# Mask table by matrix products instead of a round trip through DRAM, one full-array pair fewer, a new order table

## The chip, the core and the metric

The kernel runs on one core of one Trainium2 chip. The metric is the time on the device in microseconds (us). Five engines of the core work side by side, each on its own stream of instructions in order: TensorE (PE in the profile, its weight loads PEld), VectorE (DVE), ScalarE (ACT), GpSimd (POOL) and SyncE (SP). DMA transfers are issued from the queues of SP, POOL and ACT. TensorE writes its products to PSUM, eight banks of 512 float32 columns; ScalarE and VectorE take them from there to SBUF.

## The reference

Block-sparse attention is followed by an MLP block. Shapes: 4 batches, 8 heads, 768 tokens, head size 64; blocks of 32 tokens, so 24 blocks.

```python
scores = q @ k.T / 8
mask = |blk_i - blk_j| <= 1, or either block is the first or the last,
       or blk_j is one of 3 sampled blocks of blk_i
attn = softmax(where(mask, scores, -1e9));  x = attn @ v        # heads side by side: [4, 768, 512]

a1 = alpha1 * x + beta1
u = x + lam * (w_tok @ a1)                                     # w_tok: 768 x 768, over tokens
a2 = alpha2 * u + beta2
out = u + lam * (relu(a2 @ w_ch1) @ w_ch2)                     # 512 -> 2048 -> 512
```

The mask is the same for all batches and heads, and constant in each block of 32 x 32.

## The kernel before, in words

The 32 heads are worked in 16 pairs p (four per batch). Scores are made transposed, keys on the partitions, so that the values can be multiplied without a transpose of the attention. The scores of a pair are cut into nine units of 1024 PSUM columns; unit n = 9p + u. The kernel knows two ways to work a pair:

- **Full-array pairs**, p < NPE (5 before). The two heads go one after the other. Queries and keys are transposed on TensorE (`H`) and copied from PSUM (`hq`, `hk`) into `qx` and `kx`. Under the 64 rows of the head lie 24 more rows (`MB`, partitions 64 to 87): in `kx` an indicator of the token's block, in `qx` 0 or -400 for each block. A product over 88 rows (L585) gives score and mask at once, and the exponential of a masked score becomes 0.
- **Paired heads**, p >= NPE. Both heads are transposed by DMA (`tq`, `tk`, `dma_start_transpose` on SP) into one tile, head 0 on rows 0 to 63, head 1 on rows 64 to 127. A unit is four products over 64 rows (L595), two in each half of the array. The mask is laid on after the exponential: `m` (L613) takes the minimum of the exponentials and a table `maskT` of 0 and 65504, on VectorE.

The table `maskT` (128 x 3 x 768, f16) is made from the 24 mask rows in `qx[3]`: `M` (L493) turns them into 0 and 65504, `N` (L499) writes them to DRAM with each row 16 times, `O` (L506) reads the result back so that each partition gets its rows.

The order of all work is written out by hand in `ORDER`, a table of words that a search made. Each word issues one step, and every engine executes its share in that order (`pin_order`). The letters: `lq lk lv` loads of a pair (POOL), `F` and `held` marks that hold a load back until VectorE has passed a point, `cq ck cv` casts, `q` scores (word `q52:0`: unit 52, PSUM pair of banks 0), `e` exponential (L606, ScalarE), `m` minimum, `p` and `r` values (L619), `n` and `nt` normalisation (full-array and paired), `a b` scale and shift, `k` the token mixing (L721), `x` its addition (L730), `u U v` the transposed input of the MLP, `f` first MLP product (L787), `g` its Relu (`:a` on ScalarE L801, `:d` on VectorE L803), `h` second MLP product (L821), `o` last addition (L831), `s` store. `W w` transpose the token weights, `L S P B` prepare parameters, `z` (defined, but not in the table before) is a product of zeros that nobody reads. An engine's suffix is `:a` or `:d`.

Before the table runs a fixed opening: TensorE multiplies zeros (`zero`, L299), the first heads are transposed and the mask rows made.

Of the kernel before, what the change touches and what calls it, by code (L numbers as in the profile page):

```python
# [12 lines left out]
F16 = mybir.dt.float16  # L13
# [25 lines left out]
NPE = 5  # L39
# [19 lines left out]
r35 q39:3 e39 q36:0 k4:3 L2 x2 F27 lx1 e36 n7 ah6 q42:3 k5:2 e42 q37:2 ah7 bh7 bh6 B0 k6:0 q40:3 u2
x4 x5 e37 U1:2 e40 ck5:d k7:1 u5 u4 x6 u6 x7 q38:2 U2:7 p36:3 v1:a e38 u7 q41:0 v2:d U3:2 q43:3 p37  # L60
p38 e41 e43 v3:d f10:2 f11:5 f8:0 f14:4 g11:a g8:d S4 g14:a f9:5 f15:6 f12:1 S5 g10:d f30:7 f13:2
f31:0 f28:4 g9:a cq6:a S7 S6 g13:d g12:a g28:d g30:d f29:1 p39 p40 f2:2 g29:d f27:7 lx0 f26:4 cq5:a
S1 S0 g15:a lv5 lk6 g2:a f5:6 f24:5 f6:1 f25:2 tq5 tk5 N0 tq6 g5:a n8 g31:d g26:d f4:0 f3:6 f7:3
f0:4 g4:a cq8:a P4:a F28 S2 g24:d S3 ck6:d g25:d g3:a g6:d g27:a g0:d f16:2 f22:0 r40:5 r41 O0 lv8
g7:d F29 r42 r43 lq9 r44 g16:d g22:d f23:4 q52:0 n9 e52 tk7 tk6 q48:1 g23:d q47:3 tq7 f19:5 g19:d
e48 f1:4 a4 q53:0 e47 q51:1 f20:5 f17:6 f18:7 b4 g1:d e51 m51 cv5:d F30 lv6 k9:4 cv6:d e53 g20:a
g17:a lk9 g18:a m52 cv7:a m53 k8:5 x9 F31 x8 m47 cq9:a lv9 f21:0 q50:1 q49:3 e50 q45:2 e45 p51:1 p52
lq10 e49 g21:a p53 m48 lk10 P2:d F32 ck9:d ck8:a h0:3 nt17 F33 p48:2 P0:d m49 h1 m50 h2 tk8 q46:3
q58:2 q59:0 e46 e59 m45 p49 h3 p50 lv10 e58 u8:a ck10:a h4:6 cq10:a tq8 nt16 m46 h8:7 p45:4 p46 p47
tk9 m59 o0 P5:d h9 nt15 a5 m58 q62:0 q61:2 q56:1 h5 h10 h11 e62 m62 F34 F35 lq11 lk11 P7:d e61 e56  # L70
q57:2 s0 e57 q55:1 q60:0 F36 b5 tq9 cq11:d u9:d lv11 e60 o2 e55 m56 cv8:a h6 lq12 m57 h7 p57:7 p58
F37 m60 o1 F38 m61 p59 q54:2 q70:0 P6:d q69:1 e54 k10:6 ck11:d lk12 x10 F39 e69 e70 p60:5 m54 F40
nt19 m69 F41 p61 p62 h20:4 h21 nt20 lv12 q66:3 q65:0 q64:1 s2 m70 k11:5 m55 P3:a s1 tk10 tq10 U4 e65
x11 e66 e64 u10:a p54:0 p55 ck12:d p56 h22 nt18 q68:3 q67:0 a6 q76:1 p69:5 h23 p70 e68 b6 lq13
cq12:d m66 k13:7 e67 e76 m68 m67 p66:6 u11:a q63:1 q71:0 p67 lk13 p68 o5 F42 U5 tq11 tk11 k12:4 e63
h24:2 m65 m64 e71 x13 m63 x12 m71 nt22 h25 p63:7 u13:a ck13:a cv9:d p71 p64 s5 p65 lv13 cq13:a lq14
h26 nt23 F43 lk14 nt21 q78:0 q74:2 q72:3 a7 b7 h27 e78 e72 e74 k15:3 k14:6 x15 x14 u15:d h16:4 u12:a
u14:a U6 h17 ck14:a P1:d o6 cv10:d m74 h18 h19 q75:1 q80:0 q81:3 F44 F45 o4 lv14 U7 f45:5 f47:4 e80
e75 m80 g47:d lq15 f44:0 f46:1 f40:2 m78 g45:d g46:d g40:a e81 f43:4 f42:5 g43:d g42:a f41:1 q77:1
q79:3 q73:2 m75 F46 g44:a g41:d F47 m72 f33:0 f34:1 e79 g33:d f38:6 e77 m76 p75:7 f37:2 e73 m77 m73  # L80
g37:a p72:0 p76 p77 g34:d f52:5 f48:2 p73 p78:1 nt25 m79 g48:a g52:d p74 p79 g38:a p80 q86:1 q91:2
nt26 q82:3 e86 f54:1 nt24 e91 f59:0 s6 tq12 tk12 e82 g54:d cv11:d q89:1 m86 q85:2 f51:1 g59:d m81
e85 e89 lk15 g51:d f49:7 g49:d m85 cq15:d f56:0 f35:6 g56:a g35:a s4 f36:2 q84:2 q87:3 m91 m82 q83:0
g36:a lv15 f57:2 f53:3 e87 f39:6 f58:7 e84 e83 g57:a a8 g53:d m84 m83 g58:a m87 g39:a f55:5 g55:a
f63:0 g63:d f60:7 f32:6 p81:1 p82 p84:0 p85 g32:d g60:a p86 nt28 q98:3 q92:1 q93:2 e98 p83 nt27 m89
b8 f62:0 e93 e92 g62:a f61:6 f50:1 g50:d m98 g61:d m92 h36:7 h37 q88:1 q94:2 e94 e88 q90:0 e90 h38
h32:6 k17:4 p87:5 m93 m94 m88 x17 p88 p89 h33 q95:1 q96:0 nt29 a9 b9 cv12:a e95 e96 m95 k16:4 p93:2
x16 m90 k18:3 x18 p94 q105:2 q100:0 p95 p90:3 p91 e100 e105 p92 nt31 nt30 m105 h34 q97:0 ck15:d
q102:1 q107:2 h39 e97 m96 k19:0 m97 o9 p96:1 e102 x19 e107 tk13 tq13 s9 m102 p97 q110:1 q103:2 e110
p98 h35 nt32 p105:7 e103 q104:1 q99:0 o8 u16:a e99 a10 u18:d m103 q101:2 e101 e104 cv13:d b10 m99  # L90
u17:a m104 h40:6 h41 h42 h43 p102:4 p103 p104 q106:0 q111:1 h52:5 m101 o10 m107 m100 u19:a s8 k20:6
# [11 lines left out]
m121 k25:6 m130 p120:4 p121 p122 x25 h69 h70 h71 m133 nt40 a13 x24 b13 q131:3 q126:2 q128:0 u24:a
e131 k26:2 e128 k27:6 h88:7 x26 o17 e126 cv15:a m131 q129:1 q140:2 q136:0 e129 u26:d e140 e136 x27
m126 m129 h89 h90 p129:6 p130 p131 q127:2 m128 m136 nt43 e127 m127 q134:1 q132:0 h91 h84:5 u25:d
p126:4 o22 s17 p127 s22 e134 e132 p128 nt42 q138:3 q135:1 q142:0 h85 e138 m132 p132:4 h86 p133 e135
m134 e142 p134 U12 q137:3 q143:1 q141:0 m138 m140 nt44 h80:4 h87 m135 a14 m142 u27:a e137 m137 e143
e141 p135:6 p138:7 p136 q139:1 p137 b14 k28:0 m141 e139 m143 k29:2 p141:1 m139 nt45 x29 x28 p139
# [82 lines left out]
def kernel(  # L191
# [111 lines left out]
    for _ in range(2):  # L303
        zero(P, 6)
# [181 lines left out]

    rows = maskT[:, 0, :]

    @on("M")
    def _(_i):
# [393 lines left out]
```

## Time and profile before

| | us |
|---|---|
| median of 3 runs (lowest, highest) | 308.25 (306.98, 310.96) |
| profiled execution | 308.12 |
| its span, first to last instruction | 306.3 |
| TensorE busy | 297.5 |
| VectorE busy | 221.7 |
| ScalarE busy | 197.7 |
| GpSimd busy | 52.4 |

The span is taken from one profiled execution; the profiled execution's own time is 1.8 us longer than its span. Busy time is the union of the bars of an engine. The bars of consecutive matmuls overlap, and so do those of consecutive instructions of VectorE and ScalarE, so that the distance from start to start is the better price of an instruction in a row of its kind. "Idle before" in a group's line is the time in which the engine had nothing running ahead of these instructions, with what ended it.

### The profile page before, as it was taken

What the parts mean: (1) busy time and instruction counts of PE and PEld (TensorE: products, weight loads), DVE (VectorE), ACT (ScalarE), POOL (GpSimd) and SP (SyncE); (2) the same over time, 40 slices, a digit from 0 to 9 for tenths busy, and PEclk for the clock granted to TensorE, in tenths of its full rate; (3) what the DMA queues carried; (4) which work ended last, traced back from release to release, by engine and by line L of the source; (5) the groups of instructions that cost most, each with busy time, mean ns of one, the idle gap of its engine ahead of it and who ended that gap; (6) DMA issues with size and microseconds to landing.
All of it is one profiled execution on the core that took longest, in us unless ns stands there. A gap on an engine that the chain in (4) does not pass through costs nothing.

```text
span 306.3 us, 7729 instructions
## 1 busy us (share of the span) xinstructions
PE 297.5 (97%) x3267; PEld 193.3 (63%) x3294; DVE 221.7 (72%) x478; ACT 197.7 (65%) x259; POOL 52.4 (17%) x95
## 2 busy tenths in 40 slices
PE   8999999999999999999999999999999999999995
PEld 3677888665655675575667575656676675565443
DVE  4498999697879997789788983477888896234042
ACT  4899998837979985679767834558377861351200
POOL 4645653211425421202000000000000000000000
PEclk9999999999999999999999999999999999999999
DMA  6999999999998999533020236104010212300022
GB/s 150 173 242 217 153 202 205 185 184 173 145 144 163 206 100 184 97 89 52 3 54 2 80 67 151 57 7 55 2 36 35 62 28 44 113 2 0 0 103 105
DMA packets 48399, 31.18 MB, mean 102 GB/s; under 512 B 29020, under 2 KB 44140, under 8 KB 48364
## 3 DMA queue, kind: packets, MB, share of 16 engines
q0 software_dynamic: 16016, 15.47, 34.0%
q1 hardware_dynamic: 32132, 14.97, 22.5%
q8 instruction: 26, 0.43, 0.6%
q10 hardware_dynamic: 216, 0.24, 0.2%
q14 instruction: 9, 0.07, 0.1%
HBM read 31.45 MB, written 6.88 MB: 125 GB/s over the span
## 4 chain that ended last, share of the span: by engine, by line
PE 84%; DMA 9%; DVE 3%; issue 2%; ACT 1%; DVEq 0%; SPq 0%; ACTq 0%
PE psum L821 24%; PE psum L787 23%; PE psum L619 11%; PE psum L721 10%; PE psum L595 8%; PE psum L585 6%; DMA kx<-rel 3%; DMA v<-in_v_dram 3%; DMA uT<-ub 2%; PE psum L336 1%; DMA k2f<-in_k_dram 1%; ACT eT L606 1%; DVE x_sb L730 1%; DMA out_dram<-ot 1%; PE psum L462 0%
## 5 line engine op out<-in xcount | busy, mean ns | idle before, releaser
L606 ACT ACTIVATE eT<-psum 128x1024 f16<-128x1024 f32 x145 | 137.6, 1020 | 24.3 <-PE psum L595 19.0
L787 PE MATMUL psum<-uT,w1b 128*128 128x384 bf16 (+1 forms) x512 | 87.4, 326 | 0.5 <-DMA uT<-ub 0.4
L821 PE MATMUL psum<-w2b,hts 128*128 128x512 bf16 (+1 forms) x373 | 85.5, 370 | 1.7 <-issue 0.5
L787 PEld LDWEIGHTS <-w1b 128*128 128x128 bf16 x512 | 48.8, 98 | 34.4 <-issue 0.9
L613 DVE TENSOR_TENSOR eT<-eT,maskT 128x1024 f16<-128x1024 f16 x99 | 65.2, 684 | 5.3 <-ACT eT L606 5.0
L821 PEld LDWEIGHTS <-hts 128*128 128x128 bf16 x400 | 36.5, 98 | 37.4 <-issue 2.3
L801 ACT ACTIVATE hts<-psum,b1t 128x384 bf16<-128x384 f32 x64 | 35.1, 586 | 32.6 <-PE psum L787 31.6
L803 DVE TENSOR_SCALAR hts<-psum,b1t 128x384 bf16<-128x384 f32 x64 | 38.0, 613 | 20.9 <-PE psum L787 20.2
L619 PEld LDWEIGHTS <-eT 128*128 128x128 f16 x1152 | 43.3, 97 | 9.4 <-issue 1.7
L619 PE MATMUL psum<-vext,eT 128*128 128x65 f16 x1152 | 47.0, 193 | 0.0
L721 PE MATMUL psum<-a1p,wtokT 128*128 128x128 bf16 x576 | 36.3, 219 | 0.0
L831 DVE TENSOR_TENSOR ot<-x_sb,psum 128x512 f32<-128x512 f32 (+1 forms) x25 | 16.5, 662 | 27.0 <-PE psum L821 22.0
L721 PEld LDWEIGHTS <-wtokT 128*128 128x128 bf16 x576 | 33.4, 98 | 4.0 <-issue 1.3
L595 PE MATMUL psum<-qx,kx 64*128 64x256 bf16 x396 | 28.6, 271 | 0.6 <-DVE flag L420 0.3
L585 PE MATMUL psum<-qx,kx 88*128 88x512 bf16 (+1 forms) x120 | 26.9, 340 | 0.8 <-issue 0.6
L595 PEld LDWEIGHTS <-kx 64*128 64x128 bf16 x396 | 16.2, 94 | 11.6 <-issue 4.7
L730 DVE TENSOR_TENSOR x_sb<-x_sb,psum 128x384 f32<-128x384 f32 x32 | 17.3, 550 | 6.9 <-PE psum L721 6.7
L385 ACT CAST ub<-x_sb 128x384 bf16<-128x384 f32 x16 | 8.1, 519 | 17.3 <-DVE x_sb L730 12.8
L403 POOL DMA_DIRECT2D k<-in_k_dram x15 | 10.8, 719 | 28.8 <-DVE vext L387 10.8
L691 DVE TENSOR_TENSOR a1p<-x_sb,a_bc 128x768 bf16<-128x768 f32 (+1 forms) x17 | 15.3, 908 | 0.3
L654 DVE TENSOR_TENSOR x_sb<-psum,rcp 128x256 f32<-128x256 f32 x33 | 14.0, 424 | 1.1
L403 POOL DMA_DIRECT2D v<-in_v_dram x16 | 11.6, 728 | 13.3 <-ACT rel L385 6.6
(70 smaller groups left out, 162.0 us busy)
## 6 DMA issues: line engine op xcount, KB each, us to landing
out_dram<-ot SPq DMA_DIRECT2D x23, 256.0 KB, 2.4
v<-in_v_dram POOLq DMA_DIRECT2D x16, 192.0 KB, 5.5
k<-in_k_dram POOLq DMA_DIRECT2D x15, 192.0 KB, 5.5
q<-in_q_dram POOLq DMA_DIRECT2D x15, 192.0 KB, 6.1
w2b<-in_moe_w_ch_dram POOLq DMA_DIRECT2D x4, 512.0 KB, 9.9
w1b<-in_moe_w_ch_dram POOLq DMA_DIRECT2D x4, 512.0 KB, 11.6
wtk<-in_moe_w_tok_dram POOLq DMA_DIRECT2D x3, 384.0 KB, 10.3
mask_rows<-maskT SPq DMA_DIRECT2D x1, 576.0 KB
```

Source lines behind the costliest of these rows:

```text
L403: nc.gpsimd.dma_start(t[:], pair_ap(src, *batch(p)))
L585: nc.tensor.matmul(t[:, f : f + w], kx[h][0:KC, ts(jt, P)], qx[h][0:KC, c : c + w], start=True, stop=True,)
L595: nc.tensor.matmul(t[:, (2 * a + j) * TH : (2 * a + j + 1) * TH], kx[h][r, ts(2 * g + j, P)], qx[h][r, ts(th, TH)], start=True, stop=True,)
L606: nc.scalar.activation(eTs[n][:, c], t[:, c], AF.Exp, bias=EXPB, scale=SCALE)
L613: nc.vector.tensor_tensor(out=e, in0=e, in1=mask, op=ALU.min)
L619: nc.tensor.matmul(ops[key][:, t * VW : t * VW + D + 1], eTs[n][:, c : c + P], vext[n // NU % NV][:, a, jt, 0 : D + 1], start=(first and z ...
L721: nc.tensor.matmul(t[:, j, :], wtokT[:, s, ts(3 * g + j, P)], a1p[p][:, s, :], start=(s == 0), stop=(s == NT - 1),)
L730: nc.vector.tensor_tensor(out=sl, in0=sl, in1=tps.pop(i), op=ALU.add)
L787: nc.tensor.matmul(hps[i][:, 0:w], w1b[:, dk, ts(f, P)], uT[b][:, dk, hf * HS : hf * HS + w], start=(dk == 0), stop=(dk == 3),)
L801: nc.scalar.activation(hts[kk][:, f, :], t[:, 0:HS], AF.Relu, bias=b1t[:, f : f + 1], scale=1.0)
L803: nc.vector.tensor_scalar(out=hts[kk][:, f, :], in0=t[:, 0:HS], scalar1=b1t[:, f : f + 1], scalar2=0.0, op0=ALU.add, op1=ALU.max,)
L821: nc.tensor.matmul(cps[i][:, 0:w], hts[kk][:, nk, ts(m, P)], w2s[0][:, nk, lo : lo + w], start=(nk == 0), stop=(nk == 15),)
```

## The change

`NPE` becomes 4, so pair 4 is worked as paired heads. `M`, `N`, `O` and the DRAM tensor go. In their place `Y` multiplies, for each of the three key groups g, the indicator rows of `kx[3]` (24 x 128) with the mask rows of `qx[3]` (24 x 768) into PSUM (512 + 256 columns); `y` copies the result into `maskT`, on ScalarE as Relu(164 x + 65504), on VectorE as before. In the new table all three `y` stand on ScalarE. The opening has two more zero products of 128 columns, and the table has six `z` (three of 480, two of 256, one of 384 columns). The order table is another one throughout: it has nine more `m` (108), 43 groups of paired `q` in a row in place of 36, ten `g` more on ScalarE (74 of 128), two heads less through `H`, two more DMA transposes.

```diff
-NPE = 5
+NPE = 4
 ...
-    for _ in range(2):
+    for _ in range(4):
         zero(P, 6)
 ...
-    mask_dr = nc.dram_tensor("mask_rows", [S // 2, S], F16, kind="Internal").ap()
 ...
-    rows = maskT[:, 0, :]
-
-    @on("M")
-    def _(_i):
-        nc.vector.tensor_scalar(
-            out=rows[MB, :], in0=qx[3][MB, :], scalar1=-1.0, scalar2=F16MAX, op0=ALU.is_ge, op1=ALU.mult
-        )
-
-    @on("N")
-    def _(_i):
-        nc.sync.dma_start(
-            mask_dr.rearrange("(m i) w -> m i w", m=NBLK),
-            rows[MB, :].unsqueeze(1).broadcast_to([NBLK, BLK // 2, S]),
-        )
-
-    @on("O")
-    def _(_i):
-        nc.sync.dma_start(maskT[:], mask_dr.rearrange("(p g) w -> p g w", p=P))
+    @on("Y")
+    def _(g, j):
+        ups["Y", g] = t = psum[:, 2 * j * 512 : 2 * j * 512 + S]
+        for c, w in ((0, 512), (512, S - 512)):
+            nc.tensor.matmul(
+                t[:, c : c + w], kx[3][MB, ts(2 * g, P)], qx[3][MB, c : c + w], start=True, stop=True
+            )
+
+    @on("y")
+    def _(g, eng):
+        t = ups.pop(("Y", g))
+        if eng == "a":
+            nc.scalar.activation(maskT[:, g, :], t, AF.Relu, bias=F16MAX, scale=164.0)
+        else:
+            nc.vector.tensor_scalar(
+                out=maskT[:, g, :], in0=t, scalar1=-1.0, scalar2=F16MAX, op0=ALU.is_ge, op1=ALU.mult
+            )
```

The old table begins

```
lv0 lk1 lq1 lt1 q1:1 cq0 lq2 q2:0 q0:3 H1:5 hm0 hq1:d hk1:d e1 e0 cv0:d lv1 lk2 q3:1 q4:3 p0:5 cq1:d
```

and the new one, with its words around the mask table and the first paired units,

```
lv0 lq1 lk1 q0:2 cq0 q1:0 e0 lt2 q2:3 hm0 H1:2 lk2 e1 q3:2 hk1:d lq2 hq1:d e3 lt0 cv0:d z480:3
z480:3 z480:3 q8:0 e2 lv1 z256:2 q4:2 q5:1 cq1:d lt1 e4 F18 p0:7 p1 lq3 p2 p3 e8 p4 q7:2 ck1:d lv2
...
H7:0 L0 hk6:d lc4 e22 q16:3 lv4 p21 hk7:d e16 Y0:1 lw1 a0 p22 r22:5 r23 y0:a Y1:3 hq7:d r16 y1:a
...
n5 e30 q35:0 x1 q27:1 cq5:d e35 k0:5 b1 ck4:d e27 tk4 q31:3 x0 q33:0 e31 a2 k2:2 tq4 u0 e33 q32:3 u1
x2 q34:2 tq5 e32 q28:0 ck5:d k3:3 u2 e28 b2 U0:7 e34 x3 p27:1 p28 tk5 u3 p29 cv4:a p30 v0:d p31 U1:0
n6 r31:5 r32 v1:a r33 ah6 r34 r35 F23 bh6 lv7 q43:1 n7 q40:3 e43 k5:4 q42:0 lx1 B0 ah7 e40 lw3 bh7
...
m36 p41 e38 u6 p36:2 p37 u7 e45 q52:0 F24 m38 lq8 U3:3 e52 v3:d q47:2 lx0 p38 f12:3 e47 f15:0 g12:d
```

More of the change, by code (lines that the diff above doesn't have):

```diff
@@ L59 @@
[L59 to L91, printed above, removed]
@@ L103 @@
[L103 to L108, printed above, removed]
```

94 lines of the change are left out of this document (63 added, 31 removed).

## The prediction

> **What bounds the kernel.** First the page's busy lines, then busy time by stretch.
>
> ```profile
> PE 297.5 (97%) x3267; PEld 193.3 (63%) x3294; DVE 221.7 (72%) x478; ACT 197.7 (65%) x259; POOL 52.4 (17%) x95
> ...
> DMA  6999999999998999533020236104010212300022
> ```
>
> ```profile
> 7.00:32.00 25.00, 24.09 (x314) 17.51 (x313) 19.32 (x44) 23.59 (x28) 13.51 (x23) 1.00 1.17 208
> 32.00:57.00 25.00, 25.00 (x398) 20.36 (x396) 21.89 (x56) 22.35 (x25) 11.60 (x19) 1.00 1.12 183
> 57.00:82.00 25.00, 24.51 (x227) 15.38 (x224) 21.83 (x51) 17.67 (x32) 6.27 (x13) 1.00 1.22 178
> ```
>
> The columns after the length are TensorE, its weight loads, VectorE, ScalarE, GpSimd, clock, DMA share, GB/s. TensorE (PE) looks full everywhere, but each matmul's bar overlaps the next, so bars can't say what work is left out. I therefore read its timeline by starts.
>
> ```profile
> 6.97 2.77 PE L585 MATMUL psum<-qx,kx 88*128 88x512 bf16 x8
> 9.53 0.85 PE L336 MATMUL psum<-identb,rel 128*128 128x128 bf16 x6
> ...
> 167.51 0.66 PE L619 MATMUL psum<-vext,eT 128*128 128x65 f16 x16
> 168.10 0.61 PE L595 MATMUL psum<-qx,kx 64*128 64x256 bf16 x8
> 168.65 0.42 PE L619 MATMUL psum<-vext,eT 128*128 128x65 f16 x8
> ...
> 169.76 0.41 PE L619 MATMUL psum<-vext,eT 128*128 128x65 f16 x8
> 170.11 0.83 PE L595 MATMUL psum<-qx,kx 64*128 64x256 bf16 x12
> 170.87 0.82 PE L821 MATMUL psum<-w2b,hts 128*128 128x512 bf16 x3
> ```
>
> Starts of undisturbed steps give the price of each word of the order table: q of a full-array pair 0.436 us, q of a paired one 0.219, eight value matmuls 0.244, k 1.005, f 0.650, h 0.863 (0.437 at 256 columns), six transposes 0.335. Times their counts: f 128 steps 83.2, h 92 and 8 steps 82.9, values 35.1, k 32.2, q 99 x 0.219 = 21.7 and 45 x 0.436 = 19.6, transposes of 19 heads and tiles 6.4: 281.0 us. The first q starts at 6.97, the last matmul is over at 302.4, so 295.4 us hold 281.0 of work and **14.4 lost**. TensorE is the bound, and there are two losses to follow.
>
> The first 4.0 are lost before 56.4. The first three q's take 2.56 us from 6.97 (0.853 each, half speed), and ScalarE (ACT) cannot keep up:
>
> ```profile
> 10.86 15.79 ACT L606 ACTIVATE eT<-psum 128x1024 f16<-128x1024 f32 x17 [0.42 <-PE psum L585]
> ...
> 24.68 6.65 ACT L606 ACTIVATE eT<-psum 128x1024 f16<-128x1024 f32 x7
> ```
>
> One exponential e runs 0.916 us start to start in a row, unbroken here. Ahead of the table's word k0 stand 24 e's and a copy of 0.68: 22.7 us of ScalarE against 19.6 us of TensorE, a lead of 3.1. TensorE reached k0 at 30.42, having lost 30.42 - 6.97 - 19.6 = 3.8. So **lost = ScalarE's lead + 0.8** while ScalarE has no rest.
>
> The other 10.5 come later, most at changes between paired q (64 rows) and other work (128 rows). Sixteen values should take 0.49 and take 168.10 - 167.51 = 0.59; two q's should take 0.44 and take 0.55. Over the trace the change costs 0.095 each way: 36 groups of paired q, 72 changes, 6.8 us.
>
> **The change, part by part.**
>
> The mask by DRAM goes: M (0.35 us of VectorE, DVE), N and O (0.84 and 0.36 us of SP's queue, 576 KB each way). No row waits for maskT, because the first min comes at 77.6; TensorE gains nothing. If that cover were gone it would be the transfers' time: N was issued at 63.49, O at 70.62.
>
> In their place Y, three times 512 + 256 columns: 216 + 109 = 0.325 us each by the starts of those widths, 1.0 us of TensorE. The nearest row on 24 rows, L346 at half speed, has 0.51 for 384 columns, so 3.1 us is the other end; both lie under ScalarE's lead. The three copies y are all on ScalarE: 768 columns lie between 0.494 (512) and 0.916 (1024): 0.70 each (1.5 to 2.7 for three), 2.1 us, unhidden where ScalarE leads. Relu brings no load of tables: the trace has one such load in all, though exponentials and Relus alternate from 55 on. The six z stand while e's are awaited: 2336 columns, 1.0 us, in time that is lost anyway; without that cover they cost 1.0, or 1.9 at half speed. The two extra zero(128) (0.107 each) go into a gap of 0.39 (4.37 to 4.76) in which rel is awaited: nothing.
>
> Pair 4 becomes paired: 9 x (0.436 - 0.219) = 2.0 and twelve transposes (0.7) leave TensorE; four copies of 0.48 and two normalisations of 0.66 leave VectorE, three of 0.52 come, and so do nine mins:
>
> ```profile
> L613 DVE TENSOR_TENSOR eT<-eT,maskT 128x1024 f16<-128x1024 f16 x99 | 65.2, 684 | 5.3 <-ACT eT L606 5.0
> L595 PE MATMUL psum<-qx,kx 64*128 64x256 bf16 x396 | 28.6, 271 | 0.6 <-DVE flag L420 0.3 <-DVE x_sb L730 0.2
> L585 PE MATMUL psum<-qx,kx 88*128 88x512 bf16 x60 | 21.2, 397 | 0.8 <-issue 0.6 <-ACT eT L606 0.2
> ```
>
> 9 x 0.602 (start to start) = 5.4. The new table moves ten g's and some copies from VectorE to ScalarE, so VectorE's sum stays: 208.9 before, 208.4 after; ScalarE's goes from 185.8 to 190.4. TensorE's becomes 281.0 - 2.0 - 0.7 + 1.0 + 1.0 = 280.3. GpSimd issues the same loads in another order, with three more held copies (0.3 each); no entry of the list of waits has TensorE waiting for a load now.
>
> Two DMA transposes are added on SP, tk4 and tq4, with tq5 and tk5 behind them. Their first casts are done where the table's sum for TensorE is 28.4, so tk4 goes out near 28.4 + 6.97 + 3.9 = 39.3; the first word that needs both, q43, stands at 35.4 and comes near 46.3. Rows for such a transfer:
>
> ```profile
> 60.80 1.31 SPq L554 DMA_TRANSPOSE qx<-rel  x1
> 62.23 1.21 SPq L554 DMA_TRANSPOSE kx<-rel  x1
> ...
> 64.44 4.97 SPq L554 DMA_TRANSPOSE qx<-rel  x1
> ```
>
> They land 4.4 to 7.4 after the issue, and the chain of waits holds one for 8.24 (from 62.23). So tq4, issued one issue (1.3) later at 40.6, lands between 45.0 and 49.4: it costs 0 to 3.1. N's 576 KB, which stood between 62.23 and 64.44, are not there at 40; I take 0.
>
> **The sum.** Ahead of v3 the new table has 49 e's, three y's, one cv and one v on ScalarE: 48.4, against 44.9 of TensorE, a lead of 3.5, so 4.3 lost, and v3 comes at 6.97 + 44.9 + 4.3 = 56.2 with 235.4 left. Before, the same rest stands at 56.5: **-0.3**. In the rest 95 paired q's come in groups with 69 changes against 72: **-0.3**. At the end the two last adds follow each other, and the second waited 0.23 for an output buffer; now only one follows the last matmul: **-0.2**. Span 306.3 - 0.8 = 305.5. The profiled execution took 308.12, 1.8 more than its span (the median shown is 308.25), so **307.3 us**. The 17 changes of row count that the new table has ahead of v3 I cost at nothing, since ScalarE sets that stage; without that cover they are 17 x 0.095 = 1.6.
>
> Against the change speaks a rule of the Trainium skill (TensorEngine Tiling, Key Properties): a change of tiling mode, not merely of tile, drains TensorE. The 0.095 agrees. By the rule the Y's, on 24 rows, might each drain too, up to six changes or 0.6 us; no row here shows it, and the sum would be 307.9 if ScalarE's lead did not hide it.
>
> **Rivals.**
>
> Late transposes: q43 waits for tq4 at the long landing, and k, h and f behind it wait too. For it: a DMA share of 1.12 in that stretch. Against: no mask transfer beside it. 307.3 + 3.1 = 310.4.
>
> VectorE becomes the bound, the slower side: between the words H7 and lx0 (20.1 to 45.1 of TensorE's sum) it holds 31.4 us by mean durations, against 25.0. Before, its densest stretch (g4 to q56) held 25.7 against 20.0, yet TensorE lost only 2.1 from 70 to 90, as VectorE's operations overlap when none waits (a min takes 0.684, the next starts after 0.602). If the 6.4 are paid in full, 2.5 of them are in the sum already (ScalarE's lead grows from 1.0 to 3.5 there): 307.3 + 3.9 = 311.2. It decides from the point where the mins wait for their e's one by one, so that the overlap ends: with 0.602 per min and like prices for the rest the stretch holds 27.1, 2.1 over TensorE and less than ScalarE's 2.5; at the full prices VectorE is ahead of ScalarE.
>
> The clock opens sooner: the q's at 6.97 run at full speed. TensorE saves 3 x (0.853 - 0.436) and 0.05 on each of six transposes, 1.5, but ScalarE still sets the stage and starts 0.4 sooner: 306.9. The longer run of zeros speaks for it, a gap before rel against it. The Trainium skill (TensorE: Matmul & The Clock Gate, Part 1) has full speed after about 3.4 us of sustained work; here 3.2 us of zeros (1.19 to 4.37) did not bring it, and 3.4 might.
>
> The new table removes half of the losses, of 4.3 and 10.5: 307.3 - 7.4 = 299.9. Nothing in the sums shows where.
>
> The change may also do nothing: that the table comes early is worthless if pair 4 gains no time; that is 308.1.
>
> **Numbers.** Forecast 0.52 (306.3 to 309), which takes in doing nothing; late transposes 0.20; VectorE 0.18; clock 0.06; losses halved 0.04. The range reaches to the long landing and VectorE's price above, and below to the clock and 3 us more for a halved early loss and the spread of the runs (306.98 to 310.96): 303.8 to 312.0. A measurement tells about 2% here (302.1 and 314.4). Faster: 0.05, the last rival and a little; slower: 0.06, late transposes and VectorE at full price together (314.2) and a little; the same 0.89.
>
> **What would show it.** Right: first q near 7, v3 near 56, about 86 changes of 0.095, e's unbroken to 55. Wrong: TensorE idle ahead of q43 on kx or qx (transposes); VectorE at 95% from 28 to 55 with values waiting for mins (VectorE); q at 0.43 from 7 us on (clock); a span that differs after 57 by more than 1 us with none of these.

## The result, and the profile after

The changed kernel is slower: 311.89 us median of four runs (310.77 to 312.60) against 307.75 (four runs, 306.98 to 310.96) of the kernel before on the same chip, a ratio of 1.0132 with the 95% interval 1.0087 to 1.0177. Forecast were 307.3 us, 0.8 less than the profiled execution of before, and no difference of 2%. The profiled execution took 310.77 us with a span of 309.0, where the sum had 305.5. Line numbers of the changed kernel are one lower than before from L371 on, and two lower from L510 on (e is L604, paired q L593, f L785, h L819; full-array q L583).

The busy lines and the DMA line of the page of the changed kernel:

```profile
PE 298.5 (97%) x3308; PEld 191.7 (62%) x3308; DVE 221.6 (72%) x480; ACT 200.9 (65%) x269; POOL 53.8 (17%) x98
...
DMA  6999999999997996450167035520010022400012
```

Busy time by stretch, with the columns as before (TensorE, weight loads, VectorE, ScalarE, GpSimd, clock, DMA share, GB/s):

```profile
7.00:32.00 25.00, 24.40 (x350) 17.60 (x347) 19.32 (x49) 24.96 (x29) 15.21 (x24) 1.00 1.17 204
32.00:57.00 25.00, 23.87 (x410) 18.97 (x409) 23.72 (x53) 23.30 (x27) 8.13 (x14) 1.00 1.10 168
57.00:82.00 25.00, 23.49 (x189) 14.41 (x189) 20.89 (x53) 16.61 (x37) 9.00 (x17) 1.00 1.20 175
```

TensorE was full from 32 to 57 before; now 1.13 us of that stretch are bare of any matmul, and 1.51 of the next (0.49 before). Its timeline, read by starts as in the prediction, says where:

```profile
6.44 1.47 PE L583 MATMUL psum<-qx,kx 88*128 88x512 bf16 x8 [0.33 <-DVE qx L356]
7.75 0.50 PE L336 MATMUL psum<-identb,rel 128*128 128x128 bf16 x6
...
45.39 0.61 PE L593 MATMUL psum<-qx,kx 64*128 64x256 bf16 x8 [0.94 <-DMA qx<-rel]
...
58.70 4.08 PE L785 MATMUL psum<-uT,w1b 128*128 128x385 bf16 x24 [0.97 <-DMA w1b<-in_moe_w_ch_dram]
63.32 0.99 PE L785 MATMUL psum<-uT,w1b 128*128 128x384 bf16 x5 [0.54 <-DVE flag L419]
...
128.19 0.99 PE L785 MATMUL psum<-uT,w1b 128*128 128x384 bf16 x5 [0.76 <-ACT w1b L748]
...
158.90 1.47 PE L819 MATMUL psum<-w2b,hts 128*128 128x512 bf16 x6 [0.76 <-DVE ot L829]
```

These are five waits that the kernel before did not have (the idle time in brackets; start to start each loses some 0.17 more, and "loses" below counts that): q43 for its DMA transposes, f12 for the loaded weights, f19 for a bank that VectorE frees late (VectorE had waited 0.72 for w2b), f34 for a parameter step on ScalarE, h40 for an output buffer. The full-array q's run at 0.436 us from the first on (three in 6.44 to 7.75): the clock is open early. The groups that answer to those shown of before:

```profile
L611 DVE TENSOR_TENSOR eT<-eT,maskT 128x1024 f16<-128x1024 f16 x108 | 71.3, 685 | 7.9 <-ACT eT L604 7.7
L593 PE MATMUL psum<-qx,kx 64*128 64x256 bf16 x432 | 31.1, 271 | 0.9 <-DMA qx<-rel 0.9
L583 PE MATMUL psum<-qx,kx 88*128 88x512 bf16 (+1 forms) x96 | 20.0, 326 | 0.7 <-DVE qx L356 0.3
```

Work is as counted: nine more units of paired q, nine more mins. By the price of each word the changed table holds 280.34 us of TensorE (280.3 forecast) between 6.44 and 305.36, so 18.6 are lost, against 14.4 before and 14.5 forecast. The loss at the word f19 (63.3) is 7.6, where before it was 4.0 at 62.6; behind it 11.0 are lost against 10.5.

The queue of SP in the changed kernel, then that of GpSimd, around the first two waits:

```profile
37.22 1.32 SPq L552 DMA_TRANSPOSE kx<-rel  x1
38.65 3.46 SPq L552 DMA_TRANSPOSE qx<-rel  x2
42.21 1.97 SPq L552 DMA_TRANSPOSE kx<-rel  x1
```

```profile
34.01 0.57 POOL L444 DMA_DIRECT2D w1b<-in_moe_w_ch_dram  x1
44.57 0.34 POOL L400 COPY held<-flag 1x1 bf16<-1x1 bf16 x1 [9.99 <-DVE flag L419]
45.05 0.70 POOL L402 DMA_DIRECT2D v<-in_v_dram  x1
45.74 0.77 POOL L450 DMA_DIRECT2D w2b<-in_moe_w_ch_dram  x1
46.49 1.10 POOL L444 DMA_DIRECT2D w1b<-in_moe_w_ch_dram  x2
```

The four transposes tk4, tq4, tq5, tk5 are issued from 37.2 to 44.2; before, the first stood at 60.80. The load lv7 is held until VectorE passes the mark F23, 9.99 us long, and lx1, lw3, lw0, lx3 stand behind it on GpSimd's queue. So the last two weight loads for f (w1b) go out at 46.5, behind 512 KB of w2b, and land 9.6 and 11.5 us after their issue. f12 could start at 57.5 and starts at 58.7. In the kernel before, GpSimd's queue had them out by 38.1:

```profile
36.41 1.64 POOL L445 DMA_DIRECT2D w1b<-in_moe_w_ch_dram  x3
```

### The profile page after: what moved, and what is told of

Read it like the earlier page. It is cut to its first block, busy times and chain, and to the rows that moved or that the text cites. A ratio compares the mean times of both kernels' runs of the same rounds, so it can differ in the third digit from the quotient of the medians.

```text
span 309.0 us, 7798 instructions
## 1 busy us (share of the span) xinstructions
PE 298.5 (97%) x3308; PEld 191.7 (62%) x3308; DVE 221.6 (72%) x480; ACT 200.9 (65%) x269; POOL 53.8 (17%) x98
## 4 chain that ended last, share of the span: by engine, by line
PE 69%; DVE 6%; DMA 2%; ACT 1%; issue 0%; ACTq 0%; DVEq 0%; SPq 0%
PE psum L785 24%; PE psum L819 24%; PE psum L719 7%; PE psum L617 7%; PE psum L593 6%; DVE eT L611 2%; DMA kx<-rel 1%; DVE a1p L689 1%; DMA uT<-ub 1%; DVE x_sb L728 1%; DVE x_sb L652 1%; DVE ot L829 1%; DVE a1p L695 0%; ACT w1b L748 0%; DVE ub L386 0%
## 5 line engine op out<-in xcount | busy, mean ns | idle before, releaser
L604 ACT ACTIVATE eT<-psum 128x1024 f16<-128x1024 f32 (+1 forms) x145 | 136.9, 1029 | 38.9 <-PE psum L593 37.6
L819 PE MATMUL psum<-w2b,hts 128*128 128x512 bf16 (+1 forms) x400 | 90.9, 371 | 0.8 <-DVE ot L829 0.8
L785 PE MATMUL psum<-uT,w1b 128*128 128x384 bf16 (+1 forms) x512 | 86.7, 326 | 2.4 <-DMA w1b<-in_moe_w_ch_dram 1.0
L611 DVE TENSOR_TENSOR eT<-eT,maskT 128x1024 f16<-128x1024 f16 x108 | 71.3, 685 | 7.9 <-ACT eT L604 7.7
L785 PEld LDWEIGHTS <-w1b 128*128 128x128 bf16 x512 | 49.0, 98 | 37.5 <-issue 2.2
L799 ACT ACTIVATE hts<-psum,b1t 128x384 bf16<-128x384 f32 x74 | 40.7, 581 | 30.3 <-PE psum L785 29.5
L819 PEld LDWEIGHTS <-hts 128*128 128x128 bf16 x400 | 36.1, 98 | 37.5 <-issue 3.0
L617 PEld LDWEIGHTS <-eT 128*128 128x128 f16 x1152 | 42.3, 97 | 10.7 <-issue 2.3
L801 DVE TENSOR_SCALAR hts<-psum,b1t 128x384 bf16<-128x384 f32 x54 | 31.9, 613 | 22.9 <-PE psum L785 21.9
L617 PE MATMUL psum<-vext,eT 128*128 128x65 f16 x1152 | 46.2, 193 | 0.3 <-ACT eT L604 0.3
L593 PE MATMUL psum<-qx,kx 64*128 64x256 bf16 x432 | 31.1, 271 | 0.9 <-DMA qx<-rel 0.9
L593 PEld LDWEIGHTS <-kx 64*128 64x128 bf16 x432 | 17.6, 94 | 10.6 <-issue 5.8
L400 POOL COPY held<-flag 1x1 bf16<-1x1 bf16 x30 | 10.4, 348 | 74.4 <-DVE flag L419 74.4
L583 PE MATMUL psum<-qx,kx 88*128 88x512 bf16 (+1 forms) x96 | 20.0, 326 | 0.7 <-DVE qx L356 0.3
L652 DVE TENSOR_TENSOR x_sb<-psum,rcp 128x256 f32<-128x256 f32 x36 | 15.3, 424 | 1.2
L402 POOL DMA_DIRECT2D v<-in_v_dram x16 | 11.6, 724 | 10.5 <-DVE rel L386 5.1
```

The costliest lines, as they stand in the source:

```text
L402: nc.gpsimd.dma_start(t[:], pair_ap(src, *batch(p)))
L583: nc.tensor.matmul(t[:, f : f + w], kx[h][0:KC, ts(jt, P)], qx[h][0:KC, c : c + w], start=True, stop=True,)
L593: nc.tensor.matmul(t[:, (2 * a + j) * TH : (2 * a + j + 1) * TH], kx[h][r, ts(2 * g + j, P)], qx[h][r, ts(th, TH)], start=True, stop=True,)
L604: nc.scalar.activation(eTs[n][:, c], t[:, c], AF.Exp, bias=EXPB, scale=SCALE)
L611: nc.vector.tensor_tensor(out=e, in0=e, in1=mask, op=ALU.min)
L617: nc.tensor.matmul(ops[key][:, t * VW : t * VW + D + 1], eTs[n][:, c : c + P], vext[n // NU % NV][:, a, jt, 0 : D + 1], start=(first and z ...
```

## The experiments

The theory: the change costs what it was costed at, and the slowdown is made of waits for transfers that the new order puts late. The rivals: the three y's on ScalarE, the opening, or the fourth paired pair as such.

**The transpose earlier (a_tq).** The issue of tq4 moves in the table from behind k2 to right behind Y2.

```diff
-L1 Y2:0 lk7 e26 lw2
+L1 Y2:0 tq4 lk7 e26 lw2
...
-e31 a2 k2:2 tq4 u0 e33
+e31 a2 k2:2 u0 e33
```

> The changed kernel with one word moved: tq4, the DMA transpose of pair 4's queries, goes out right after the third product Y2 instead of after tk4 and k2. Late-transfer theory (the changed kernel is slow because transfers that its new table needs earlier land late): TensorE's wait of 1.1 us ahead of q43 and ScalarE's rest of 1.6 us at 45.8 vanish, and the time falls by 1.1 to 1.6 us against the changed kernel (ratio to before 1.008 instead of 1.013). Changes-of-row-count theory (the 17 changes and 6 of the Y's ahead of v3 are not hidden and cost 2.2 us): the wait vanishes but the time falls by 0.5 us at most. If tk4 lands later than tq4, the wait stays as it is under both.

Measured 313.59, 1.0179 (1.0137 to 1.0221): no gain, rather a loss. tq4 went out at 26.32, but q43 then lost 0.84 to kx, whose transpose tk4 still went out at 38.8: the wait stays, as the expectation allowed for a late tk4. It did not foresee the loss. In this profile the mark F23 is passed 1.0 us later than in the changed kernel, the two w1b loads go out 1.0 later, f12 loses 2.92 to them, and 6.83 us of half speed lie around the end of that wait. What makes the mark late is not shown.

**The weight loads earlier (a_w1).** lw3 and lw0 right behind lw2, ahead of the mark.

```diff
-lk7 e26 lw2 q29:1
+lk7 e26 lw2 lw3 lw0 q29:1
...
-ah7 e40 lw3 bh7 m43 q44:1 lw0 e42
+ah7 e40 bh7 m43 q44:1 e42
```

> The changed kernel with two words moved: lw3 and lw0, the last two loads of w1b, go out right after lw2 instead of behind the load lv7 that waits 10 us for a mark of VectorE. Late-transfer theory: issued near 35 instead of 46.5, w1b is there before f12, TensorE's wait of 1.0 us ahead of f12 vanishes and the time falls by about 1.0 us. Rival (the DMA engines are full until 100 us, share 1.1, so that an earlier load only pushes back another): the wait moves to a later load (v of pair 4, k of pair 5) and the time stays within 0.5 us.

Measured 316.12, 1.0277 (1.0230 to 1.0324). The wait of f12 went, as wanted, but the transposes now stand behind the weights. SP's queue and TensorE of this kernel:

```profile
38.65 9.12 SPq L552 DMA_TRANSPOSE qx<-rel  x2
```

```profile
49.16 1.04 PE L593 MATMUL psum<-qx,kx 64*128 64x256 bf16 x8 [4.70 <-DMA qx<-rel]
...
58.92 0.94 PE L593 MATMUL psum<-qx,kx 64*128 64x256 bf16 x8 [2.60 <-DMA kx<-rel]
```

The issue of tq4 and tq5 took 9.12 us in place of 3.46, q43 waited 4.70 and a later paired q 2.60. Neither expectation held: the time rose. With the weights issued first, the transposes wait; from 44.0 to 48.8 us the DMA engines are at a share of 1.21. Another place for the two loads, behind the transposes but ahead of the mark, was not tried. And around the end of each of the two long waits a stretch of TensorE at half speed begins, to which the last section comes back.

**The y's on VectorE (a_yd).** `y0:a y1:a y2:a` become `y0:d y1:d y2:d`.

> The changed kernel with the three copies y on VectorE instead of ScalarE. If ScalarE sets the pace from 7 to 57 us, as the sums of the prediction have it, its 2.1 us of y's go straight into the time: f12 starts about 2 us earlier and the time falls by 1 to 2 us, as far as the late transfers then do not hold q43 and f12 longer. If TensorE sets the stage with its changes of row count, nothing falls (0 to +0.5 us, since VectorE takes 2.1 us more).

Measured 313.11, 1.0188 (1.0151 to 1.0225). VectorE comes to them later; three full-array q's that reuse a bank wait for the copy on L502, idle 0.46, 0.47 and 0.58 us. q43 loses 1.72. Both branches of the expectation missed. Moving the y's off ScalarE does not help; what they cost there this run can't tell, since the new waits cover it.

**The opening alone (b_z4).** The kernel before with four zero products in place of two.

```diff
-    for _ in range(2):
+    for _ in range(4):
         zero(P, 6)
```

> The kernel before with four zero products of 128 columns in its opening instead of two, as the changed kernel has. In the profile of the changed kernel TensorE ran at full speed from 4.6 us on, in that of before from 10.3 us. If the two zeros bring this, the profile here shows the clock at full speed from about 4.6 us, the first q near 6.4 with 0.44 us per q, and the time falls by 1 to 2 us. If it is the phase of a free-running window, the profile may show either, and the median falls by less than 0.5 us.

Measured 308.00, 1.0014 (0.9985 to 1.0042). The clock opened at 5.40 us in place of 10.26, and the first q's ran at 0.44 us each; the time stayed, where the expectation had 1 to 2 us less. That fits the sum of the prediction, in which ScalarE sets that stage.

**The broadcast loads left out (a_nolc, b_nolc).** In both kernels the loads of alpha1, beta1 and alpha2 are replaced by ones that GpSimd writes.

```diff
+        if 0 < i < 4:
+            nc.gpsimd.memset(t[:], 1.0)
+            return
```

> The changed kernel with less for the DMA engines early: the broadcast loads of alpha1, beta1 and alpha2 (256 KB each, between 15 and 27 us) are left out, and GpSimd writes ones there, so these parameters are not the given ones. Nothing else moves. DMA-room theory (the DMA engines are full until 60 us, four transposes take 8 us of them from 38 on, and q43 and f12 wait for what comes late): 0.77 MB less are about 4 us of DMA work at 190 GB/s, so the waits ahead of q43 (1.1) and f12 (1.0) vanish or halve, and the time falls by 1.5 to 3 us (ratio to before about 1.004 to 1.008). If the loads are late only because the load lv7 waits for its mark, f12's wait stays and the time falls by 1 us at most. If TensorE's changes of row count or ScalarE's copies are the cause, nothing falls.

> The control for it: the kernel before with the same three broadcast loads left out (ones written by GpSimd instead). In before no work of TensorE waits for a load ahead of 57 us, its first transposes by DMA go out at 60.8. All theories: ratio 0.997 to 1.003.

Measured: the changed kernel 310.72, 1.0091 (1.0060 to 1.0123); the kernel before 308.87, 1.0018 (0.9978 to 1.0057). With fewer bytes ahead, f12 no longer waits; q43 still loses 1.46 and f19 1.23. The control stayed, as expected; the changed kernel's gain is below the expected one, and its interval overlaps that of the changed kernel. So bytes are part of f12's wait, and q43's does not hang on them.

**The four weight loads together behind lv7 (a_lw).** The order on GpSimd's queue becomes lv7, lw3, lw0, lx3, lx1, all still behind the mark F23.

```diff
-F23 bh6 lv7 q43:1 n7 q40:3 e43 k5:4 q42:0 lx1 B0 ah7 e40 lw3 bh7 m43 q44:1 lw0 e42 x5 k4:7 u5 lx3 e44
+F23 bh6 lv7 lw3 lw0 lx3 lx1 q43:1 n7 q40:3 e43 k5:4 q42:0 B0 ah7 e40 bh7 m43 q44:1 e42 x5 k4:7 u5 e44
```

> The changed kernel with four loads in another order behind lv7: lw3 and lw0 (the rest of w1b) first, then lx3 and lx1 (w2b), instead of lx1, lw3, lw0, lx3. They go out at the same time as in the changed kernel, after the transposes of pairs 4 and 5. DMA-room theory: w1b lands earlier by about one load of 512 KB (2 to 2.6 us), f12's wait of 1.0 us vanishes, q43's stays, and the time falls by about 1 us, to a ratio near 1.010. Rival: S2 on VectorE, which needs lx1, now holds f19 longer (0.7 us now), and nothing is won.

Measured 309.40, 1.0062 (1.0026 to 1.0099), span 306.8. GpSimd's queue and TensorE of this kernel:

```profile
45.01 0.35 POOL L400 COPY held<-flag 1x1 bf16<-1x1 bf16 x1 [9.98 <-DVE flag L419]
...
46.19 1.10 POOL L444 DMA_DIRECT2D w1b<-in_moe_w_ch_dram  x2
47.27 1.52 POOL L450 DMA_DIRECT2D w2b<-in_moe_w_ch_dram  x2
```

```profile
45.24 0.61 PE L593 MATMUL psum<-qx,kx 64*128 64x256 bf16 x8 [0.34 <-DMA qx<-rel]
...
57.16 0.42 PE L617 MATMUL psum<-vext,eT 128*128 128x65 f16 x8
57.54 2.79 PE L785 MATMUL psum<-uT,w1b 128*128 128x385 bf16 x16
```

The waits of f12 and f19 are gone although the two w1b loads go out only 0.3 us earlier: 512 KB of w2b no longer stand ahead of them, and they land 5.9 and 7.8 us after their issue in place of 9.6 and 11.5. The gain is larger than expected; f19's wait went too. It was measured again beside the changed kernel (c_lw below).

**Pair 4 transposed on TensorE (a_pet, a_pet_lw).** tq4 and tk4 go; six plus six transposes (A, as in the opening) and two copies on VectorE (D) take their place, without and with the loads' move of a_lw (there A8 stands ahead of A9).

```diff
-ck4:d e27 tk4 q31:3
+ck4:d e27 q31:3
...
-k2:2 tq4 u0
+k2:2 u0
...
-e34 x3 p27:1 p28 tk5
+e34 x3 A9:4 D9:d p27:1 p28 A8:6 D8:d tk5
```

> The changed kernel with pair 4 transposed on TensorE (twelve transposes into PSUM, 0.7 us, and two copies of 0.5 us by VectorE) instead of by DMA; it stays a paired pair. DMA-room theory: two of the four early DMA transposes go (about 4 us of the DMA engines), q43 waits for nothing, pair 5's transposes and w1b come earlier, f12's wait vanishes, and the time falls by 1.5 to 2.5 us (ratio near 1.006). If paired work of pair 4 costs more than the sums say for another reason (mins on VectorE, changes of row count), the time stays or rises by up to 1 us.

> The changed kernel in the better order of loads (ratio 1.006), with pair 4 transposed on TensorE instead of by DMA. DMA-room theory: q43's wait (0.5 to 1.1 us) goes, against 0.7 us of transposes and 1.0 us of copies on VectorE, which has no room there either: ratio 1.003 to 1.008. If the profile has the clock open near 14 us again, as in the run without the new order of loads, about 1.5 us are due to that.

Measured 313.76, 1.0195 (1.0121 to 1.0270), and 310.05, 1.0062 (1.0030 to 1.0094). The second is no better than a_lw at 1.0062: q43's wait goes, but the transposes wait 0.80 for a bank that e frees, and two U's behind them wait 0.34 and 0.20 for VectorE. So q43's wait was not bought off with TensorE's time here. a_pet missed its expectation: f12 still waits, 1.74 us. (Its profile has the clock opening at 13.97 us; its lowest run, 312.93, is still above the changed kernel.)

**All waits that the profile names (a_best).** a_lw, and two late moves: the stores s6 and s4 ahead of tq12 on SP's queue, P0 on VectorE.

```diff
-f45:4 m76 P0:a f41:0
+f45:4 m76 P0:d f41:0
...
-q90:3 m89 m78 tq12 h34 e79 p81:2 s6 tk12
+q90:3 m89 m78 s6 s4 tq12 h34 e79 p81:2 tk12
...
-nt28 s4 m79 q92:0
+nt28 m79 q92:0
```

> The changed kernel with w1b's rest ahead of w2b as in the run before it (ratio 1.006), and with two later waits taken away: the stores s6 and s4 go out on SP ahead of tq12, which held them back until 153 us so that o8 and h40 waited (0.95 us), and P0 is on VectorE, so that f34 does not wait for ScalarE, which stands behind a cast held by a DMA transpose (0.57 us). Theory that the loss is a sum of such single waits: the time falls by another 1.3 to 1.5 us, to a ratio of 1.001 to 1.002. If a wait removed there is only paid at the next step, it stays near 1.006.

The reason for the late moves is in SP's queue of the changed kernel: the stores stand behind the transpose tq12. That one waits 27.6 us, until 152.5, for q79, the last product that reads the tile it writes. So the buffer that o8 needs, and with it h40, comes late.

```profile
152.51 1.21 SPq L552 DMA_TRANSPOSE qx<-rel  x1
153.82 0.53 SPq L838 DMA_DIRECT2D out_dram<-ot  x1
```

Likewise f34 waits for P0 on ScalarE, which stands behind the cast cq14, and that waits 2.57 us for a DMA transpose to release its tile. Measured 308.28, 1.0018 (0.9987 to 1.0049): as fast as the kernel before, no faster.

**The two edits apart and together, beside the changed kernel.** The four corners on one chip, against 308.91 us of the kernel before: c_after is the changed kernel as it stands, c_lw has the loads' move alone, c_late the late moves alone, c_both both.

> The changed kernel unchanged, beside the other three corners. Theory of two separate causes (loads behind lv7 near 45 us, queue waits near 127 and 158 us): 1.011 to 1.014. Rival, that the differences between earlier calls were the chip and the call: 1.005 to 1.008, like the loads' move alone.

> The four weight loads directly behind lv7, nothing else. Theory of two separate causes: 0.006 to 0.008 below the changed kernel of this call (the two waits of 1.0 and 0.7 us at 57 and 62 us gone, some half-speed windows with them). Rival: no more than 0.003 below it.

> Only the later moves: the stores s6 and s4 ahead of tq12, P0 on VectorE in place of ScalarE. Theory of two separate causes: the waits of 0.9 us ahead of f34 and 0.9 us ahead of h40 go, 0.004 to 0.006 below the changed kernel of this call, and the wait of 1.0 us ahead of f12 stays. Rival: the late waits only move to the next word that needs the same transposes, 0 to 0.002 below it.

> Both edits. Theory of two separate causes: their gains add, 0.010 to 0.013 below the changed kernel of this call, within 0.003 of the kernel before. Rival, that each edit removes a loss that the other would have hidden: no more than the better of the two alone.

| | median us | ratio to the kernel before (95%) |
|---|---|---|
| c_after | 312.23 | 1.0105 (1.0056 to 1.0154) |
| c_lw | 309.60 | 1.0029 (0.9993 to 1.0065) |
| c_late | 310.44 | 1.0062 (1.0026 to 1.0099) |
| c_both | 308.52 | 1.0010 (0.9976 to 1.0045) |

The loads' move takes away 0.0076 and the late moves 0.0043, each as expected; both take 0.0095, just short of the 0.010 expected. Their sum would be 0.0119, which the intervals can't tell from 0.0095. Each of the two gains by itself, and together they make up nearly all of the 0.0105; that their gains add up in full is not shown, for the step from c_lw to c_both, 0.0019, is within the noise. TensorE's timelines of c_late (line numbers one lower again) and of c_both:

```profile
62.30 4.08 PE L784 MATMUL psum<-uT,w1b 128*128 128x385 bf16 x24 [1.31 <-DMA w1b<-in_moe_w_ch_dram]
...
126.78 8.13 PE L784 MATMUL psum<-uT,w1b 128*128 128x384 bf16 x49
```

```profile
45.38 0.61 PE L593 MATMUL psum<-qx,kx 64*128 64x256 bf16 x8 [0.57 <-DMA qx<-rel]
...
57.66 10.66 PE L785 MATMUL psum<-uT,w1b 128*128 128x385 bf16 x64
```

c_late keeps f12's wait and has 49 f products in a row where f34 had waited; c_both has 64 in a row from f12 on, and keeps a wait of 0.57 ahead of q43.

**The mask products alone (b_Y).** The kernel before, still with five full-array pairs, gets Y and y near 50 us in place of M, N and O.

```diff
-p31 e32 M0 a2
+p31 e32 a2
...
-e40 ck5:d k7:1 u5 u4 x6 u6 x7 q38:2
+e40 ck5:d Y0:3 k7:1 Y1:2 y0:a u5 u4 x6 Y2:3 y1:a u6 x7 y2:a q38:2
...
-f25:2 tq5 tk5 N0 tq6
+f25:2 tq5 tk5 tq6
...
-r40:5 r41 O0 lv8
+r40:5 r41 lv8
```

> The mask part alone: the kernel before with its own table and five full-array pairs, in which M, N and O are replaced by the three products Y and three copies on ScalarE, put near 50 us. TensorE has 1.0 us of products and six changes of row count (0.6) more; ScalarE's 2.1 us fall where it has rest; SP and the DMA engines lose two transfers of 576 KB at 63 to 75 us, beside the first DMA transposes. If the products are what makes the changed kernel slow: ratio 1.005. If the time of TensorE is all that counts: +1.6 us at most, less what the freed transfers give back at the waits near 81 us (0.9 us): ratio 1.000 to 1.005.

Measured 310.48, 1.0056 (1.0019 to 1.0093). TensorE's loss by 60 us grew from 3.9 to 7.4. In it are 3.41 us at half speed from 54.56 and, as these lines of TensorE's timeline show, waits that come from the place of the words and not from their price:

```profile
51.44 0.49 PE L492 MATMUL psum<-qx,kx 24*128 24x512 bf16 x2 [0.78 <-ACT eT L604]
...
54.37 0.88 PE L583 MATMUL psum<-qx,kx 88*128 88x256 bf16 x3 [0.58 <-ACT maskT L500]
```

So the products bring nothing by themselves to a kernel whose mask by DRAM was not waited for. How much of the 1.7 us is their work and how much their place is not separated. Five of the twelve runs have a mean clock of 0.994, as one such half-speed stretch would give; their median is 311.06, that of the other seven 309.28.

**The four pairs without the products (a_dram).** The order of a_lw, the mask through DRAM as before: M and N at Y0's place, O at y2's.

```diff
-p21 hk7:d e16 Y0:1 lw1 a0 p22 r22:5 r23 y0:a Y1:3 hq7:d r16 y1:a
+p21 hk7:d e16 M0 N0 lw1 a0 p22 r22:5 r23 hq7:d r16
...
-L1 Y2:0 lk7
+L1 lk7
...
-k1:4 y2:a n5
+k1:4 O0 n5
```

> The changed kernel in the better order of loads (ratio 1.006), with the mask table through DRAM again: M and N in the place of Y0, O near the place of y2, so four full-array pairs without the products. ScalarE has 2.1 us less in the stage that it paces, TensorE 1.6 us less. DMA-room theory: two transfers of 576 KB at 28 to 45 us take room from the loads and stand on SP ahead of pair 4's transposes, so q43 waits longer, by 2 us or more, and the time is the same or longer (ratio 1.006 to 1.015). If ScalarE's copies were what the four-pair table pays for: 1.5 to 2 us less (ratio near 1.000).

Measured 333.22, with four runs so far apart (322.72 to 334.73) that no interval is given. SP's queue and TensorE:

```profile
30.23 0.81 SPq L499 DMA_DIRECT2D mask_rows<-maskT  x1
44.50 0.35 SPq L506 DMA_DIRECT2D maskT<-mask_rows  x1
45.03 1.33 SPq L554 DMA_TRANSPOSE kx<-rel  x1
46.48 13.33 SPq L554 DMA_TRANSPOSE qx<-rel  x2
```

```profile
64.98 1.04 PE L595 MATMUL psum<-qx,kx 64*128 64x256 bf16 x8 [20.16 <-DMA qx<-rel]
```

O waits until N has landed, 13.4 us, and holds the transposes up behind it on SP's queue: q43 waits 20 us. The sign is as expected, the size far beyond it. With the transposes of the first paired heads due near 37 us, the trip through DRAM at this place is dear, and the products avoid it; in the kernel before, with these transposes from 60.8 us on, it was free. O behind the transposes was not tried.

## Why the prediction was wrong, point by point

The span came out 3.5 us above the forecast sum (309.0 against 305.5). By the profiled execution: the first q 0.5 early (-0.5); up to q47 at 56.99, 5.65 lost in place of 4.3 (+1.35); from there to f19, 1.9 (+1.9), nothing forecast; later 11.0 in place of 10.2 (+0.8); the tail 3.64 in place of 3.7 (-0.1).

**Right.** The prices and the sum of TensorE's work (280.3). ScalarE as the pace up to 57 us, which its timeline shows:

```profile
7.36 22.74 ACT L604 ACTIVATE eT<-psum 128x512 f16<-128x512 f32 x25
30.00 1.58 ACT L500 ACTIVATE maskT<-psum 128x768 f16<-128x768 f32 x2
...
43.40 0.80 ACT L384 COPY uT<-psum 128x768 bf16<-128x768 bf16 x1
45.83 12.94 ACT L604 ACTIVATE eT<-psum 128x1024 f16<-128x1024 f32 x14 [1.63 <-PE psum L593]
```

It is unbroken from 7.4 to 44.2, and again from 45.8 to 58.8. The three y's took 2.3 us by their starts, 2.1 forecast. The tail moved as forecast.

**Right in kind, and its cover as said.** The Y's drain TensorE: the first took 0.43 to the next start, in place of 0.325, as these lines of TensorE's timeline show.

```profile
29.22 0.49 PE L492 MATMUL psum<-qx,kx 24*128 24x512 bf16 x2
29.65 0.66 PE L617 MATMUL psum<-vext,eT 128*128 128x65 f16 x16
```

That agrees with the rule of the Trainium skill (TensorEngine Tiling, Key Properties) that a change of mode drains the array, here about 0.10 us for 24 rows as for 64. It stayed hidden under ScalarE's pace, as the forecast had it: 2.4 were lost at 42.7.

**The step that failed first: "it costs 0 to 3.1 ... I take 0".** The late transposes were the rival with 0.20. Its place and its sign came true: TensorE idle ahead of q43 on qx. The landing was within the bounds given, at their low end (45.0 forecast at best, 45.4 seen), and that is in part luck: tq4 went out at 38.65 in place of 40.6 and then took 6.7 us, where the forecast had 4.4 to 8.8. Wrong was when q43 would be due: "near 46.3", and it was due at 44.3, since the first q came 0.5 earlier and only 2.4 were lost by then, not 3.9. So what the early clock saved was lost again at q43. TensorE lost 1.11 there; ScalarE, which sets the pace, rested 1.63, and that is in the 5.65. The wait is not all of the slowdown: c_both still has 0.57 of it and is level with the kernel before.

**The step that cost most: "GpSimd issues the same loads in another order".** It was costed at nothing, since TensorE waited for no load before. The 1.9 us at f12 and f19 are its price in the profiled execution, and c_lw, which moves these loads and nothing else, gives 0.0076, 2.3 us. The prediction looked at whether anything waits for a load now, not at when each load goes out in the new order: lw3 and lw0 stand behind a marked load, and the mark F23 is passed at 44.6. The DMA share of 1.12, which the text cited in favour of late transposes, spoke for late loads just as much.

**Two losses further on that no step had.** f34 (0.93) and h40 (0.94) wait because a store and a parameter step stand in order behind a transpose or a cast that waits. c_late, which moves both, gives 0.0043, 1.3 us; the two were not tried apart. The forecast took the losses after 57 us to move with the changes of row count alone. The sum there came out 0.8 above the forecast, not 1.9, so other losses shrank.

**The other rivals.** VectorE is not the bound, though it is busy 23.72 of 25 us from 32 to 57, the 95% that the text named as its sign: the other half of that sign is missing. In that stretch the values' products (L617) wait for nothing; in the whole trace they wait 0.3 us for an e, and their weight loads 0.7 us for mins. The clock opened early, as that rival said, and b_z4 shows that this alone changes no time. Halved losses did not come.

**What the runs' clocks add.** One half-speed stretch of 3.41 us, as described below, lowers the mean clock of a run by about 0.0055 (a_pet and b_Y, with one in the profiled execution, have 0.995 and 0.994). None is in the profiled executions of the changed kernel, but a mean clock of 0.993 to 0.995 stands in two of its four runs, which are the longest (312.40 and 312.60), in two of the six of c_after, and in seven of the twelve of c_late (median 310.80; the other five 309.72). These are kernels in which f12 waits. Where the loads' move has taken that wait away (a_lw, a_pet_lw, a_best, c_lw, c_both), none of 56 runs is below 0.998; of the kernel before, 3 of 99 are at 0.994 or below. This would fit late loads that cost, in some runs, more than the 1.9 us of waiting. Where in these runs the stretch lay no kept trace shows.

**What stays open.** Whether the four-pair table could gain with q43's wait gone: c_both still has 0.57 of it, and a version without DMA transposes ahead of q43 and without new waits was not tried. What the three y's cost on ScalarE is not measured by itself either.

## What to carry to other kernels

A new order of issues is a change of its own, even where "the same loads" are issued: write down for every transfer when it goes out, what holds the queue ahead of it, and when its first reader is due, and compare that with how full the DMA engines are in that stretch. A transfer that nobody waited for was worth nothing to remove. DMA transposes that are brought forward into a stretch of loads compete with them: with two weight loads issued ahead of them (a_w1), the issue of two transposes took 9.12 us in place of 3.46. Undo the waits one at a time against the profile: here three moves of a few words brought the slower kernel level with the old one, and none beat it.

## What the runs showed of the hardware

**DMA transposes are dear.** Busy time by stretch of the changed kernel, and its queues from 36 to 52 us (MB and share of the 16 engines' time):

```profile
40.00:44.00 4.00, 4.00 (x96) 3.71 (x95) 3.75 (x10) 3.94 (x5) 0.00 (x0) 1.00 1.00 76
...
20.00:36.00 16.00, 15.68 (x238) 11.21 (x236) 13.39 (x34) 15.96 (x18) 8.90 (x15) 1.00 1.20 218
```

```profile
q0 software_dynamic: 1174, 1.49, 59.1%
q1 hardware_dynamic: 3200, 0.79, 48.1%
```

After the load at 34.01 GpSimd issues none until 45.05. So from 40 to 44 us hardly anything but the transposes is under way, and yet the DMA engines show a share of 1.00 (1.20 while loads ran) and move 76 GB/s in place of 218. From 36 to 52 us, four transposes of 196 KB (0.79 MB) hold 48.1% of 16 us, 7.7 us of all engines or 1.9 each: 102 GB/s, where the loads get 1.49 MB in 9.5 us, 158 GB/s. (The two shares add up to 107%, so the packets' times hold some waiting for each other.) The Trainium skill (Advanced Engine Details and Errata, X-Bar Transpose (TRN2)) has transposing DMAs as fast as plain ones; these runs do not agree.

**A wait of TensorE can cost twice.** Busy time of a_w1 by stretch, around the end of its wait of 4.70 us (the column of 0.50 is the granted clock):

```profile
48.80:52.20 3.40, 3.04 (x28) 2.36 (x29) 0.69 (x1) 1.94 (x2) 0.52 (x1) 0.50 1.39 189
```

In a_w1 half speed lasted 3.41 us around the end of that wait, from 48.83, and 3.41 behind the one of 2.60, from 59.07. It lasted 6.83 us in a_tq around the end of a wait of 2.76, and 20.48 in a_dram, from 48.87, inside the wait of 20.16, to 69.35. It came after shorter waits too: 3.41 us in a_pet after one of 1.74 ahead of f12, and in b_Y after those of 0.78 and 0.58. In the profiled executions none followed f12's waits of 0.97 in the changed kernel, 1.31 in c_late and 1.53 in c_after, though other runs of these kernels probably have one, as said above.

All these changes of the clock lie on a grid of 3.41 us that begins where the clock opened. In a_w1 it opened at 4.45, and half speed began 13 and 16 steps later; in b_Y 13 steps after 10.19, in a_pet 15 after 13.97, in a_tq 16 after 5.21, in a_dram 13 and 21 after 4.50. In the step ahead of the change TensorE's bars left 0.86 (b_Y) to 3.41 us (a_w1) idle, and steps with up to 1.56 us idle (a_yd) passed without one. So idle time alone does not decide. That the same kernel has a half-speed stretch in some runs only would fit a grid that lies otherwise in each run; that is not shown.

The Trainium skill (TensorE: Matmul & The Clock Gate, Part 1) names an idle window of about 3.4 us; the length of the half-speed stretches agrees, but no single wait had to be that long here.

**The opening of the clock varies.** With two zero products it opened at 10.26, 10.03 and 10.19 us (before, b_nolc, b_Y); with four, mostly between 3.9 and 6.5 us, but at 13.97 in a_pet and 13.17 in c_late. Six transposes that start at 17.29 us in c_after's profile start at 20.36 in c_late's. Of these 3.1 us, 0.45 were there before the first transposes of the opening (4.60 against 5.05, a wait for a load), so the opening at 13.17 in place of 6.26 went with some 2.6 us; one at 10.26 in place of 5.40 changed no time (b_z4 against the kernel before).
